# Attention woven into a gated MLP on one core: rounded parts ahead of the gate's functions, exponents gathered

## The chip, the cores and the metric

The kernel runs on one core of a Trainium2 chip. A core has five engines that run their own queues of instructions in order and meet at semaphores: TensorE (PE, matrix products, with its weight loads PEld), VectorE (DVE), ScalarE (ACT, functions read from tables), GpSimd (POOL) and SyncE (SP), which here issues the transfers. The metric is device time in microseconds (us) of one execution; less is better.

## The reference

Sliding-window attention over 8 batches, 8 heads, 576 positions and 64 features, half of the heads dense and half dilated, then a two-layer MLP without bias on the 4608 rows:

```python
scores = scale * np.matmul(q, k.transpose(0, 1, 3, 2))
scores = np.where(masks[None, :, :, :], scores, -1000000000.0)
scores = scores - np.max(scores, axis=-1, keepdims=True)
attn = np.exp(scores)
attn = attn / (np.sum(attn, axis=-1, keepdims=True) + 1e-09)
x = np.matmul(attn, v)          # then (batch, position, head, feature) as 4608 x 512
h = x @ w_in                    # 512 -> 2048
sp = np.maximum(h, 0.0) + np.log1p(np.exp(-np.abs(h)))
g = h * erf(sp)
out = g @ w_out                 # 2048 -> 512
```

## The kernel before

**Attention** is cut into 72 units of four blocks of 64 queries, for two heads at once. A unit passes through: `scores` (PE, 16 small products), `mask_max` (DVE, four, each with a row maximum `nmax`), `exponents` (ACT, four Exp with row sums `ssum`, and one small add on POOL), `normalize` (a reciprocal on DVE, a product on POOL), `transposes` (PE, four) and `turned` (their copy to `pT`), `values` (PE, 16 small products), and then x's two parts: `rows_hi` (ACT: the values rounded to the short matmul format) and `rows_lo` (DVE: the rest). From `scores` of unit n to `values` of unit n are three visits (`LAG = 3`): a visit scores unit n and attends unit n-3.

**The MLP** runs over nine chunks of 512 rows, each in steps of two tiles of 128 hidden features; 72 steps in all, called t. A step is done in two half steps, x = 2t + j. In half step x, PE runs `mm1` (12 products into the one bank `h`), the transposes of units that are due, `mm2` of the step two earlier (12 products into the four banks `acc`), and then values and scores of the units that are due. DVE copies `h` to `hc` (`take`) in each half step. In an odd half step ACT does Erf of the step before (`table`) and then Sigmoid and Ln of its own step (`argument`); each of Erf, Ln and Exp begins with a load of the function table (Sigmoid uses Erf's). DVE makes from Erf's result the two parts of g (`gate`) that the next two half steps' `mm2` read. Besides, weights in double precision are taken apart into two parts, one tile per half step in the first quarter (`prep_act` on ACT, `prep_dve` on DVE; each takes what the other made a half step before).

**Which half step does what** is a fixed plan, `visits()`: the units 0 to 13 are scored before the first `mm1`; 14 to 20 come one to a half step, x = 0 to 6; 21, 22 and 23 at x = 9, 11 and 14; after that two at a time at x = 18, 23, 28, 31, 34, 38, 41, 45 and so on up to 102. The order of instructions within a half step is the order of the calls in the main loop; each engine keeps it. `todo` holds units that are scored and wait for their exponents, `scaled` those that wait for `normalize`. In x = 0 to 3 there is no `mm2` yet, and the transposes come ahead of `mm1`. There the banks `acc` still serve attention: unit u has `acc[(u + 1) % 4]`, so unit 14's values (x = 3) stand in `acc[3]`, which the first `mm2` at x = 4 writes over.

In the profiled execution `mm1` of x = 0, 1, 2, 3, 4, 5 begins at 49.67, 54.09, 59.10, 66.99, 71.87 and 80.37 us, that of x = 8, 9 and 10 at 101.42, 106.86 and 113.99, and that of x = 18 at 162.14.

Of the kernel before, what the change touches and what calls it, by code (L numbers as in the profile page):

```python
# [10 lines left out]
F32 = mybir.dt.float32  # L11
# [7 lines left out]
P = 128  # L19
# [15 lines left out]
PER = 4  # L35
# [26 lines left out]
LAG = 3  # L62
# [40 lines left out]
def key_start(u, j):  # L103

    return j * BLK + (WIN if (PER * u) // NBLK != (PER * u + j) // NBLK else 0)
# [7 lines left out]
def attn_moe_kernel(ctx: ExitStack, tc: tile.TileContext, qk, v, masks, eye, w_in, w_out, out):  # L113
# [3 lines left out]
    def pool(name, bufs, space=bass.MemoryType.SB, **kw):  # L117
        return ctx.enter_context(tc.tile_pool(name=name, bufs=bufs, space=space, **kw))
# [7 lines left out]
    io, work, small = pool("io", 2), pool("work", 2), pool("small", 3)  # L126
# [47 lines left out]
    probs, maxes, sums, x_rows = {}, {}, {}, {}  # L174
# [3 lines left out]
    def scores(u):  # L178
        i = u % 2
        for j in range(PER):  # L180
            at, r = QW + key_start(u, j), j % 2 * BLK
            for h in range(2):
                hs = slice(h * D, (h + 1) * D)
                nc.tensor.matmul(sps[h][r:r + BLK, i, j // 2, :], qkz[i][hs, j * BLK:(j + 1) * BLK],  # L184
                                 qkz[i][hs, at:at + KEYS], start=True, stop=True)

    def mask_max(u):
        pr = probs[u] = work.tile([P, PER, KEYS], F32, name="prob", bufs=LAG + 1)
        nmax = maxes[u] = small.tile([P, PER], F32, name="nmax")
        for h in range(2):  # L190
            for p in range(PER // 2):
                n = PER * u + 2 * p
                nc.vector.tensor_tensor_reduce(  # L193
                    out=pr[:, 2 * h + p, :], in0=sps[h][:, u % 2, p, :], in1=mask[PAIRS.index((kind(n), kind(n + 1)))],
                    scale=-SCALE, scalar=BIG,
                    op0=ALU.add, op1=ALU.min, accum_out=nmax[:, 2 * h + p:2 * h + p + 1],
                )

    def exponents(u):
        nmax = maxes.pop(u)  # L200
        sums[u] = small.tile([P, PER], F32, name="ssum")
        for j in range(PER):
            nc.scalar.activation(  # L203
                out=probs[u][:, j, :], in_=probs[u][:, j, :], func=AF.Exp,
                scale=-1.0, bias=nmax[:, j:j + 1], accum_out=sums[u][:, j:j + 1],
            )
        nc.gpsimd.tensor_scalar(sums[u], sums[u], 1.0e-9, None, op0=ALU.add)
# [20 lines left out]
    def values(u):  # L228
        xp, vt, pt = place(u), vz[u % 2], pz[u in second]
        for j in range(PER):  # L230
            r = j % 2 * BLK
            for h in range(2):
                nc.tensor.matmul(xp[h * D:(h + 1) * D, j * BLK:(j + 1) * BLK], vt[:, j, h, :],  # L233
                                 pt[:, 2 * h + j // 2, r:r + BLK], start=True, stop=True)

    def pieces(u):

# [26 lines left out]
    def rows_hi(u):  # L264
        for hi, _, src in rows_of(u):
            nc.scalar.copy(out=hi, in_=src)  # L266

    def rows_lo(u):

        for hi, lo, src in rows_of(u):  # L270
            nc.vector.tensor_tensor(out=lo, in0=src, in1=hi.bitcast(F32), op=ALU.subtract)  # L271
        for it in [i for i in x_rows if PER * (u + 1) >= NBLK * (i + 1)]:
            b, hp = divmod(it, HP)

            at = slice(TOK if it < twice else 0, TOK if twice <= it < HP else S)

            if HP + twice <= it < 2 * HP:
                whole[it] = x_rows[it]
                at = slice(TOK - (S - TOK), S)
            a = b, hp, at, x_rows.pop(it)  # L280
            if it < HP:
                stores.append(a)
            else:
                soon(store_x, *a)
# [92 lines left out]
    def prep_dve(keep=None):  # L377

        if rest and rest[0][0] < calls[0]:
            _, w, hi, lo = rest.popleft()
            nc.vector.tensor_tensor(lo, w, hi.bitcast(F32), op=ALU.subtract)  # L383
        if begun and begun[0][0] < calls[0]:
            _, i, d, hi, lo, w = begun.popleft()
            t = w.bitcast(I32)
            nc.vector.tensor_scalar(t, t, 3, None, op0=ALU.logical_shift_left)
            nc.vector.scalar_tensor_tensor(t, d[:, :, 1], -0x80000000, t, op0=ALU.bitwise_and, op1=ALU.bitwise_or)  # L388
            nc.vector.scalar_tensor_tensor(t, d[:, :, 0], 29, t, op0=ALU.logical_shift_right, op1=ALU.bitwise_or)  # L389
            made.append((w, hi, lo))  # L390
            if i != keep:
                soon(load_w, i)
# [68 lines left out]
    def table(t):  # L461
        nc.scalar.activation(out=ls[t], in_=ls[t], func=AF.Erf, scale=-1.0)  # L462
# [66 lines left out]
    with tc.manual_schedule():  # L529
        load_qk(0)  # L530
        nc.sync.dma_start(out=cst, in_=masks)
        for t in vz:
            nc.gpsimd.memset(t[KEYS:P], 0.0)
        nc.gpsimd.memset(pz[0][KEYS:P], 0.0)
        load_qk(1)
        nc.sync.dma_start(out=ident, in_=eye)
        for n in range(FIRST):
            if n < 3:
                load_w(n)
            first_visit(n)  # L540
            if 1 <= n <= EARLY:
                prep_dve()
        normalize(FIRST - 2)
        rows_lo(FIRST - 1 - LAG)

        plan = visits()

        pause = 2 * (USED[SPC - 1] + 1) - 2

        late = 3  # L550
        todo, scaled = [], [FIRST - 1]
        for x in range(2 * (NT + 2)):
            t, j = divmod(x, 2)
            ns = plan.get(x, [])
            scored, ready = [n for n in ns if has(n)], [n - LAG for n in ns]
            second.update(ready[1:])

            if t < 2:
                turn(ready)
            if t < NT:  # L560
                after = STEPS[t + 1][0] if ends(t) and t + 1 < NT else None
                if x == 2 * HALF - 4:
                    load_x(1, range(twice))
                elif after and after > 1 and j == 0:
                    load_x(after, range(twice))
                if x in (2 * HALF - 2, SAVED):
                    hold(True)
                mm1(t, j)
                if x == 0:
                    for a in stores:  # L570
                        store_x(*a)
                if after is not None and j == PAIR - 1:
                    load_x(after, range(twice, CC))
                    hold(False)
                take(t, j)

            if j == 0 and x or x == 1:
                for u in todo:
                    exponents(u)
                scaled, todo = scaled + todo, []  # L580
            if j == 1 and 1 <= t <= NT:
                table(t - 1)
            if t >= 2:
                turn(ready)
            if j == 1 and 1 <= t <= NT:
                gate(t - 1, 0)
            if j == 0 and 2 <= t:
                gate(t - 2, 1)
            if j == 1 and t < NT:
                argument(t)  # L590
            if x != pause:
                prep_act()
            if x not in (pause, late):
                prep_dve(keep=2 if SAVED - 4 < x <= SAVED else None)
            if t >= 2:
                mm2(t - 2, j)
                if x == SAVED:
                    save()
                    hold(False)
                    load_w(2)  # L600
                elif ends(t - 2):
                    if j == 1:
                        store(STEPS[t - 2][0])
                    elif STEPS[t - 2][2] == 2:
                        fetch()
            for m in ready:
                values(m)
            for n in scored:
                scores(n)
            for n in ns:  # L610
                soon(load_qk, n + 2)
                soon(load_v, n - 1)
            for n in scored:
                mask_max(n)
                todo.append(n)
            if x == late:
                prep_dve()
            while scaled:
                normalize(scaled.pop(0))
            for m in ready:  # L620
                rows_hi(m)
            for m in ready:
                rows_lo(m)
            if x == SAVED + 2:
                nc.gpsimd.memset(pz[1][KEYS:P], 0.0)
        assert not todo and not prep and not staged and not begun and not made and not rest
# [84 lines left out]
```

## Time and profile before

| | |
|---|---|
| median of 3 runs | 943.34 us (941.51 to 943.72) |
| the profiled execution | 942.44 us, of which the span of the profile is 940.7 |
| PE busy | 915.1 us, 97% |
| ACT busy | 642.5 us, 68% |
| DVE busy | 562.2 us, 60% |
| POOL busy | 82.9 us, 9% |
| granted TensorE clock, mean | 0.997 |

PE is the engine that is nearly always busy, so what the others do counts only where PE waits. The 25.6 us in which PE does nothing are nearly all in the first 85 us. A line of the timeline gives start, duration, engine, line of the kernel, what is written and read, and in brackets how long the engine had been idle and what it waited for.

### The profile page before, as it was taken

How to read it: one execution, taken by the hardware profiler on the slowest of the kernel's cores; microseconds unless marked ns; L12 is line 12 of the kernel's file. 1: busy time of each engine (PE TensorE's matmuls, PEld its weight loads, DVE VectorE, ACT ScalarE, POOL GpSimd, SP SyncE). 2: the span in 40 equal slices, each digit the busy share in tenths (PEclk: the TensorE clock that was granted, in tenths of full speed). 3: DMA queues.
4: the chain of work that ended last, by engine and by line, in shares of the span. 5: the costliest groups of instructions: out<-in, count | busy, mean ns of one | idle time of the engine just before them, and what ended most of it. 6: DMA issues, size and time to landing. Idle time of an engine off the chain costs nothing.

```text
span 940.7 us, 15969 instructions
## 1 busy us (share of the span) xinstructions
PE 915.1 (97%) x6048; PEld 747.8 (80%) x6048; DVE 562.2 (60%) x1511; ACT 642.5 (68%) x1202; POOL 82.9 (9%) x154
## 2 busy tenths in 40 slices
PE   5789999999999999999999999999999999999998
PEld 4567887888888878888888878888888888888886
DVE  6879889886565545555665555555555444335434
ACT  7879888785866866667578657866566555445553
POOL 2321110110100100000000000100000000000000
PEclk9999999999999999999999999999999999999999
DMA  8766444432631242313232152314220302011001
GB/s 277 254 219 222 155 155 136 156 112 94 194 111 67 67 157 67 111 68 116 83 111 73 62 186 103 112 60 132 84 78 34 114 12 79 1 45 45 0 1 45
DMA packets 51500, 98.73 MB, mean 105 GB/s; under 512 B 7136, under 2 KB 20192, under 8 KB 51424
## 3 DMA queue, kind: packets, MB, share of 16 engines
q1 hardware_dynamic: 51136, 97.19, 30.9%
q8 instruction: 48, 0.79, 0.3%
q10 hardware_dynamic: 288, 0.52, 0.1%
q14 instruction: 28, 0.23, 0.1%
HBM read 69.52 MB, written 27.26 MB: 103 GB/s over the span
## 4 chain that ended last, share of the span: by engine, by line
PE 88%; DVE 6%; DMA 3%; ACT 2%; issue 1%; POOL 0%; SPq 0%; POOLq 0%; ACTq 0%; DVEq 0%
PE h L446 40%; PE acc L487 39%; PE tx L233 3%; PE sp L184 3%; PE sp L217 3%; DMA x<-xT 1%; DVE w L388 1%; DVE w L389 1%; DMA qk<-in_qk_dram 1%; DVE prob L193 1%; DVE win_lo L383 1%; PE acc L217 1%; DVE s L469 1%; DMA dbl<-in_w_in_dram 0%; DVE pT L220 0%
## 5 line engine op out<-in xcount | busy, mean ns | idle before, releaser
L454 DVE COPY hc<-h 128x512 f32<-128x512 f32 x144 | 99.5, 691 | 273.5 <-PE h L446 273.1
L446 PE MATMUL h<-x,win_hi 128*128 128x512 f32 x832 | 259.3, 393 | 0.9 <-DMA x<-xT 0.9
L487 PE MATMUL acc<-wout_hi,ghi 128*128 128x512 f32 x576 | 227.5, 395 | 1.2 <-DVE rows L271 1.0
L487 PE MATMUL acc<-wout_lo,ghi 128*128 128x512 f32 x576 | 224.4, 390 | 0.0
L458 ACT ACTIVATE s<-hc 128x1024 f32<-128x1024 f32 x72 | 76.4, 1062 | 184.4 <-DVE hc L454 184.3
L446 PEld LDWEIGHTS h<-x,win_hi 128*128 128x128 f32 x832 | 155.0, 188 | 35.2 <-issue 1.4
L446 PE MATMUL h<-x,win_lo 128*128 128x512 f32 x416 | 162.3, 390 | 0.0
L487 PE MATMUL acc<-wout_hi,glo 128*128 128x512 f32 x576 | 158.8, 389 | 0.0
L487 PEld LDWEIGHTS acc<-wout_hi,ghi 128*128 128x128 f32 x576 | 108.2, 188 | 23.6 <-DVE rows L271 1.4
L487 PEld LDWEIGHTS acc<-wout_hi,glo 128*128 128x128 f32 x576 | 108.1, 188 | 22.6
L487 PEld LDWEIGHTS acc<-wout_lo,ghi 128*128 128x128 f32 x576 | 108.3, 188 | 21.4
L203 ACT ACTIVATE prob<-prob,nmax 128x96 f32<-128x96 f32 x288 | 104.0, 364 | 5.4 <-DVE nmax L193 5.1
L473 DVE TENSOR_TENSOR glo<-s,ghi 128x512 fp32r<-128x512 f32 x144 | 99.7, 693 | 5.1
L459 ACT ACT_TABLE_LOAD x72 | 92.4, 1283 | 1.3
L462 ACT ACT_TABLE_LOAD x72 | 92.4, 1283 | 1.3
L469 DVE TENSOR_TENSOR s<-hc,s 128x1024 f32<-128x1024 f32 x72 | 88.1, 1224 | 7.1 <-ACT s L462 7.1
L446 PEld LDWEIGHTS h<-x,win_lo 128*128 128x128 f32 x416 | 78.3, 188 | 16.7
L193 DVE CUSTOM_DVE_ANT_0 prob<-sp,cst 128x96 f32<-128x96 f32 x288 | 54.8, 253 | 51.8 <-PE sp L184 51.7
L446 PE MATMUL h<-dbl,win_hi 128*128 128x512 f32 x256 | 80.7, 396 | 0.0
L266 ACT CAST rows<-tx 128x64 fp32r<-128x64 f32 (+5 forms) x116 | 26.2, 356 | 75.2 <-PE tx L233 75.2
L462 ACT ACTIVATE s<-s 128x1024 f32<-128x1024 f32 x72 | 76.5, 1062 | 0.8
L459 ACT ACTIVATE s<-s 128x1024 f32<-128x1024 f32 x72 | 76.4, 1061 | 0.8
(59 smaller groups left out, 929.2 us busy)
## 6 DMA issues: line engine op xcount, KB each, us to landing
xT<-rows SPq DMA_DIRECT2D x26, 576.0 KB, 4.7
v<-in_v_dram SPq DMA_DIRECT2D x72, 192.0 KB, 3.8
qk<-in_qk_dram SPq DMA_DIRECT2D x48, 272.0 KB, 3.9
dbl<-in_w_in_dram SPq DMA_DIRECT2D x16, 512.0 KB, 4.2
dbl<-in_w_out_dram SPq DMA_DIRECT2D x16, 512.0 KB, 3.4
qk<-in_qk_dram SPq DMA_DIRECT2D x24, 288.0 KB, 3.9
out_dram<-w SPq DMA_DIRECT2D x26, 256.0 KB, 2.3
x<-xT SPq DMA_DIRECT2D x8, 320.0 KB, 5.2
```

The source lines that it names most:

```text
L184: nc.tensor.matmul(sps[h][r:r + BLK, i, j // 2, :], qkz[i][hs, j * BLK:(j + 1) * BLK], qkz[i][hs, at:at + KEYS], start=True, stop=True)
L193: nc.vector.tensor_tensor_reduce(out=pr[:, 2 * h + p, :], in0=sps[h][:, u % 2, p, :], in1=mask[PAIRS.index((kind(n), kind(n + 1)))], scale ...
L203: nc.scalar.activation(out=probs[u][:, j, :], in_=probs[u][:, j, :], func=AF.Exp, scale=-1.0, bias=nmax[:, j:j + 1], accum_out=sums[u][:, ...
L217: nc.tensor.transpose(out=turn_place(u)[0:KEYS, j * P:(j + 1) * P], in_=pr[:, j, :], identity=ident)
L446: nc.tensor.matmul(h, w[:, cc, ft * P:(ft + 1) * P], x[cc], start=(k == 0 and i == 0), stop=(k == CC - 1 and i == 2))
L454: nc.vector.tensor_copy(out=hs[t][:, j], in_=h)
L458: nc.scalar.activation(out=ls[t], in_=hs[t], func=AF.Sigmoid, scale=-1.0)
L459: nc.scalar.activation(out=ls[t], in_=ls[t], func=AF.Ln, bias=TINY)
L462: nc.scalar.activation(out=ls[t], in_=ls[t], func=AF.Erf, scale=-1.0)
L469: nc.vector.tensor_tensor(out=e, in0=hc, in1=e, op=ALU.mult)
L473: nc.vector.tensor_tensor(out=glo, in0=e[:, j], in1=ghi.bitcast(F32), op=ALU.subtract)
L487: nc.tensor.matmul(acc[tt], g[:, tt * P:(tt + 1) * P], w[:, ft, :], start=(first and w is wout_hi and g is ghi), stop=(last and g is glo))
```

## The change

Four edits. First, a new function `attend` holds values, scores and `rows_hi`, in this order. In x = 0 to 3 it is called right behind `exponents` and `table`, ahead of `gate`, `argument` and `prep_act`; from x = 4 on it stands where values and scores stood. Second, `exponents` run only at an even x at which some waiting unit's transposes are due at x + 2 or earlier (and at x = 1), for all waiting units at once. Third, `prep_dve` of x = 3 goes behind `rows_lo`. Fourth, `nmax` and `ssum` have four buffers and not three.

```diff
-        nmax = maxes[u] = small.tile([P, PER], F32, name="nmax")
+        nmax = maxes[u] = small.tile([P, PER], F32, name="nmax", bufs=LAG + 1)
...
-        sums[u] = small.tile([P, PER], F32, name="ssum")
+        sums[u] = small.tile([P, PER], F32, name="ssum", bufs=LAG + 1)
...
+    def attend(ready, scored):
+        for u in ready:
+            values(u)
+        for u in scored:
+            scores(u)
+        for u in ready:
+            rows_hi(u)
...
+        due = {n - LAG: x for x, ns in plan.items() for n in ns}
...
-            if j == 0 and x or x == 1:
+            if x == 1 or j == 0 and any(due[u] < x + 3 for u in todo):
                 for u in todo:
                     exponents(u)
...
+            if t < 2:
+                attend(ready, scored)
             if t >= 2:
                 turn(ready)
...
-            for m in ready:
-                values(m)
-            for n in scored:
-                scores(n)
+            if t >= 2:
+                attend(ready, scored)
...
-            if x == late:
-                prep_dve()
             while scaled:
                 normalize(scaled.pop(0))
             for m in ready:
-                rows_hi(m)
-            for m in ready:
                 rows_lo(m)
+            if x == late:
+                prep_dve()
```

By the plan the exponents of units 18 and 19 move from x = 6 to x = 8, beside 20; those of 21 and 22 from x = 10 and 12 to x = 16, beside 23. Eight later pairs move by one even half step, from x = 20, 24, 42, 56, 60, 74, 88 and 92 to x + 2. The groups of exponents go from 32 to 29.

On ACT in x = 1 and 2 of before, from the exponents of unit 14 to those of unit 15 (the first line is unit 14's, `rows<-acc_94` is `rows_hi` of unit 12):

```order
L203 ACTIVATE prob,ssum<-prob,nmax 128x96 x4
L458 ACT_TABLE_LOAD
L458 ACTIVATE s<-hc 128x1024
L459 ACT_TABLE_LOAD
L459 ACTIVATE s<-s 128x1024
L369 CAST wout_hi<-w 128x512
L374 ACTIVATE w<-dbl_552 128x512
L266 CAST rows<-acc_94 128x256
L203 ACT_TABLE_LOAD
```

The same place now:

```order
L203 ACTIVATE prob,ssum<-prob,nmax 128x96 x4
L274 CAST rows<-acc_94 128x256
L466 ACT_TABLE_LOAD
L466 ACTIVATE s<-hc 128x1024
L467 ACT_TABLE_LOAD
L467 ACTIVATE s<-s 128x1024
L377 CAST wout_hi<-w 128x512
L382 ACTIVATE w<-dbl_552 128x512
L203 ACT_TABLE_LOAD
```

`rows_hi` of unit 12 has gone from behind Sigmoid, Ln and `prep_act` to the front of them.

On POOL from x = 6 to x = 16 of before (`ssum` is the add of one unit, `prob<-prob,rinv` the product of one unit; the first two rows are units 18 and 19, the four at the end 20 and 21):

```order
L207 TENSOR_SCALAR ssum<-ssum 128x4 x2
L212 TENSOR_TENSOR prob<-prob,rinv 128x384 x2
L425 CAST x_99<-x_99 128x2x64
L425 CAST x_100<-x_100 128x2x64
L207 TENSOR_SCALAR ssum<-ssum 128x4
L212 TENSOR_TENSOR prob<-prob,rinv 128x384
L207 TENSOR_SCALAR ssum<-ssum 128x4
L212 TENSOR_TENSOR prob<-prob,rinv 128x384
```

The same stretch now, with units 18 to 20 and then 21 to 23:

```order
L433 CAST x_99<-x_99 128x2x64
L433 CAST x_100<-x_100 128x2x64
L207 TENSOR_SCALAR ssum<-ssum 128x4 x3
L212 TENSOR_TENSOR prob<-prob,rinv 128x384 x3
L632 MEMSET pT_89 32x512
L207 TENSOR_SCALAR ssum<-ssum 128x4 x3
L212 TENSOR_TENSOR prob<-prob,rinv 128x384 x3
```

Three adds now stand ahead of the first of three products.

## Rows read from the trace of the kernel before

**Rows 1.** The page, busy time, share and instructions of each engine.

```profile
PE 915.1 (97%) x6048; PEld 747.8 (80%) x6048; DVE 562.2 (60%) x1511; ACT 642.5 (68%) x1202; POOL 82.9 (9%) x154
```

**Rows 2.** Busy time by stretches: PE, PEld, DVE, ACT, POOL; PEclk, DMA, GB/s.

```profile
62.00:64.80 2.80, 0.09 (x3) 0.01 (x2) 1.08 (x3) 2.78 (x5) 0.31 (x1) 1.00 0.92 327
64.80:69.00 4.20, 4.20 (x41) 3.52 (x42) 4.13 (x17) 4.17 (x14) 1.09 (x2) 0.59 0.13 39
66.00:67.00 1.00, 1.00 (x14) 0.74 (x9) 0.96 (x2) 1.00 (x6) 0.00 (x0) 0.50 0.00 0
77.00:78.00 1.00, 0.32 (x1) 0.30 (x2) 1.00 (x4) 0.99 (x2) 0.00 (x0) 1.00 0.09 12
100.00:120.00 20.00, 20.00 (x117) 16.26 (x117) 18.07 (x39) 19.04 (x36) 2.27 (x3) 1.00 0.42 143
```

**Rows 3.** PE's timeline: start, duration, line, tiles, idle before and its releaser.

```profile
57.60 0.69 PE L233 MATMUL acc<-pT,v 128*64 128x64 f32 x16 [0.51 <-DVE pT L220]
...
64.79 0.69 PE L233 MATMUL acc<-pT,v 128*64 128x64 f32 x16 [2.71 <-DVE pT L220]
...
77.68 0.50 PE L487 MATMUL acc<-wout_hi,ghi 128*128 128x512 f32 x1 [0.96 <-DVE rows L271]
...
84.09 0.64 PE L217 MATMUL sp<-ident,prob 128*96 128x128 f32 x4 [0.69 <-POOL prob L212]
```

**Rows 4.** ACT's timeline, half steps 1 to 3.

```profile
57.63 1.28 ACT L458 ACT_TABLE_LOAD   x1
...
63.33 0.36 ACT L266 CAST rows<-acc 128x256 fp32r<-128x256 f32 x1
...
69.38 1.06 ACT L462 ACTIVATE s<-s 128x1024 f32<-128x1024 f32 x1
```

**Rows 5.** DVE's timeline, half steps 1 to 4.

```profile
63.72 0.42 DVE L271 TENSOR_TENSOR rows<-acc,rows 128x256 fp32r<-128x256 f32 x1 [2.39 <-ACT rows L266]
...
71.48 1.22 DVE L469 TENSOR_TENSOR s<-hc,s 128x1024 f32<-128x1024 f32 x1
...
82.89 0.24 DVE L211 RECIPROCAL rinv<-ssum 128x4 f32<-128x4 f32 x2
```

**Rows 6.** ACT, POOL and PE around half steps 7 to 9.

```profile
99.62 1.06 ACT L458 ACTIVATE s<-hc 128x1024 f32<-128x1024 f32 x1 [1.16 <-DVE hc L454]
...
106.18 0.36 ACT L203 ACTIVATE prob<-prob,nmax 128x96 f32<-128x96 f32 x1
...
106.54 0.36 ACT L203 ACTIVATE prob<-prob,nmax 128x96 f32<-128x96 f32 x1
106.80 0.19 ACT L203 ACTIVATION_READ_ACCUMULATOR prob<-prob,nmax 128x1 f32 x1
...
107.15 0.68 POOL L207 TENSOR_SCALAR ssum<-ssum 128x4 f32<-128x4 f32 x1 [7.77 <-ACT prob L203]
...
109.58 0.60 PE L217 MATMUL sp<-ident,prob 128*96 128x128 f32 x4
```

**Rows 7.** ACT, DVE and PE in half steps 17 and 18.

```profile
159.33 1.06 ACT L462 ACTIVATE s<-s 128x1024 f32<-128x1024 f32 x1
...
160.42 1.23 DVE L469 TENSOR_TENSOR s<-hc,s 128x1024 f32<-128x1024 f32 x1 [0.27 <-ACT s L462]
...
165.75 1.27 DVE L220 COPY pT<-sp 96x512 f32<-96x512 f32 x2
...
168.40 1.15 PE L233 MATMUL tx<-pT,v 128*64 128x64 f32 x32
```

**Rows 8.** POOL and PE in half steps 30 and 31.

```profile
242.44 0.22 POOL L207 TENSOR_SCALAR ssum<-ssum 128x4 f32<-128x4 f32 x1 [1.20 <-ACT prob L203]
242.74 1.61 POOL L212 TENSOR_TENSOR prob<-prob,rinv 128x384 f32<-128x384 f32 x2
...
244.51 1.03 PE L217 MATMUL sp<-ident,prob 128*96 128x128 f32 x8
```

**Rows 9.** Line by line: the table loads ahead of Exp.

```profile
L203 ACT ACT_TABLE_LOAD x32: 1283/1283/1283, 0.7 to 705.9; - x32
```

## The prediction

> **What bounds the kernel now.** The page comes first: PE works 915.1 of 940.7 us [rows 1], so at most 25.6 us are to be had from PE's waits, and only there. Then busy time by stretches: from 100 us on PE is busy 20.00 of 20 us although ACT is at 19.04 [rows 2], so an ACT instruction saved there brings nothing by itself; it can only cost, where a result comes too late. Third, PE's timeline from the first `mm1` to x = 5: four waits, 0.51, 2.71, 0.96 and 0.69 us [rows 3]. The longest belongs to `values` of unit 13 at x = 2. It waits for `turned` on DVE, which stands behind `rows_lo` of unit 12; that waited 2.39 us for `rows_hi` [rows 5], and `rows_hi` ran at 63.33, because Sigmoid, Ln and `prep_act` had begun at 57.63 ahead of it [rows 4], although the values it reads were done at 57.60 + 0.69 = 58.29 [rows 3]. After this wait the granted clock is 0.50, the 1.2 GHz level, and over 64.8 to 69.0 it is 0.59 on the mean [rows 2]: 4.2 x (1 - 0.59) = 1.7 us lost beside the 2.7 us. The third wait, 0.96 us, is the first `mm2`, whose bank `acc[3]` `rows_lo` of unit 14 still read; the clock stays at 1.00 there [rows 2]. Behind 84.09 PE has hardly a wait; 100 to 120 us shows none [rows 2].
>
> **Edit one, x's parts first (x = 0 to 3).** The 2.71 us wait itself goes: `rows_hi` of unit 12 can start at 58.33 and `rows_lo` right behind the reciprocal, some 2.4 us earlier [rows 5]. But what is late next is ACT. Between 57.63 and the end of Erf of step 0 at 69.38 + 1.06 = 70.44 ACT is busy all the time (2.78 of 2.80 us, 4.17 of 4.20 us) [rows 2, 4]. Now this row of work begins with an instruction that must wait for `values` until 58.33, with Sigmoid, two table loads, Ln, `prep_act` and the exponents of unit 15 queued behind it. The work is the same, it starts 58.33 - 57.63 = 0.70 us later, so Erf ends at 71.14. DVE's product for `gate` of step 0 began at 71.48, held by the copy of `h`, since PE was late [rows 5]; now the copy is early and Erf is what it waits for: 71.18, a gain of 0.3 us. From there to the reciprocals at 82.89 DVE works without a pause on the same instructions in another order (edit three only moves `prep_dve`, 2.4 us, behind `rows_lo`: the 0.96 us wait of `mm2` goes, but the copy of `h` of x = 4 still comes behind both). The reciprocals release POOL's product, and this releases the transposes at 84.09, PE's last wait in this stretch [rows 3]. So they come at 83.79.
>
> PE thus loses the 2.71 and 0.96 us, and waits elsewhere: `prep_dve` of x = 2 needs what `prep_act` of x = 1 makes, now 1.07 us later (0.70, and the 0.36 of `rows_hi` that went ahead), the reciprocal of unit 15 needs exponents that end 0.7 us later, and `turned` of unit 14 is behind both. So I expect new waits for `turned`, of about 2 us each, ahead of `values` of unit 14 and, as DVE gains only 0.3 us, of unit 15. Bounds of edits one and three together: a gain of 6.1 us if all goes (2.71 + 0.96 + 0.69 + 1.7); a loss of 0.7 if the clock falls after the last of these waits: PE's work up to its wait at 84.09 ended at 84.09 - 0.69 = 83.40 [rows 3], now 0.3 earlier and 1.7 longer, 84.8. Without that PE has time until 83.79. I take the chain: **-0.3 us**.
>
> **Edit two, exponents late and together.** Three table loads of 1.283 us go [rows 9], all on ACT, at x = 6, 10 and 12. PE is without a wait there, so I count 0. What it costs, by place:
>
> x = 8, units 18, 19, 20; unit 18's transposes are due at x = 9. Sigmoid of step 3 still starts behind the copy of `h` at 99.62 [rows 6], so the exponents of x = 8 start when they did. One activation takes 0.36 us, start to start; unit 20's four ended at 106.80 + 0.19 = 106.99 [rows 6]. Eight more: 109.87. POOL begins the add 0.16 us later (107.15 behind 106.99): 110.03. The add takes 0.22 us [rows 8] to 0.68 [rows 6]; DVE is idle then, waiting for this very add, so I take 0.22. In POOL's queue the three adds stand before the three products, so unit 18's product has to wait for unit 20's add: 110.03 + 0.30 = 110.33 (from 242.44 to 242.74), and 1.61 / 2 = 0.8 us for one product [rows 8]: 111.15. The transposes stood at 109.58, without a wait [rows 6]; now 111.2: **+1.6 us**, 2.1 with the slower add. Nothing gives it back, since PE is the bound behind it.
>
> x = 16, units 21, 22, 23, due at x = 18. There is time for the transposes, but ACT is 8 x 0.36 = 2.9 us longer and Erf of step 7 stands behind: its end goes from 160.39 to 163.3. DVE's `gate` product waited for it already (0.27 us) [rows 7], and from its start at 160.42 DVE has `gate`, `prep_dve`, the copy of `h` and the two copies `turned` in one row without a pause, the latter at 165.75, two in 1.27 us. All this moves by 2.9: the copies end at 169.3 and 169.95. `values` of the two units ran at 168.40 for 1.15 us; the second half, which began near 168.97, must wait until 170.0: **+1.0 us**.
>
> The eight pairs: seven become due at the next half step. That is what before does in other places: at x = 30 and 31 the second product ends at 244.35 and the transposes start at 244.51 with no wait [rows 8], and the next even x is freed of just this load. 0 each; at x = 22, where `prep_act` still runs, up to 0.2.
>
> **Edit four**, one more buffer of 16 bytes a row for `nmax` and `ssum`: units now wait four deep, no instruction is added. 0.
>
> **Sum:** -0.3 + 1.6 + 1.0 = +2.3 us. On the profiled execution's 942.44 this is 944.7; the median of the runs is 0.9 above it, so **945.6 us**. A change below 0.3%, 2.8 us, can't be told from none here; 2.3 us is just below.
>
> **Rivals.**
>
> *The clock falls at x = 9.* The same two stalls, but PE's pause there, from about 109.7 to 111.2, halves the clock as the 2.71 us at x = 2 did: 1.7 us more, 947.3 us, slower. For it: rows 2 show the fall, and that PE pays it when it is the bound. Against: 0.96 us did not do it, and 1.5 is nearer to that. It decides somewhere between 0.96 and 2.71 us. The Trainium skill (TensorE: Matmul & The Clock Gate, section HAM oscillation — how this bites in real kernels) says that waits between bursts of matmuls drop the array to the low clock and that this is paid anew each time; by that rule every new wait is a risk, and the trace agrees for the one of 2.71 us.
>
> *The stalls are covered.* If ACT, with nothing to do at x = 6, gets ahead after all, or DVE has more slack at x = 18 than I see, only the 0.3 us stay: 943.0 us. For it: with the pairs the plan does the same without a wait [rows 8]. Against: Sigmoid at 99.62 waited 1.16 us for PE [rows 6], so time saved on ACT before it is lost.
>
> *All early waits go.* The gain is 2.71 + 0.96 + 0.69 + 1.7 = 6.1 us, less the stalls' 2.6: 939.8 us, faster. For it: PE waits there for ACT's results, and ACT is what the change relieves. Against: ACT has no gap in 62 to 69 us [rows 2], and no work is taken from it before x = 6. A page of the Trainium skill (ScalarE: Activation LUTs, sections Table sets: the hidden batching unit and What ACT_TABLE_LOAD costs) advises to gather activations by table set and prices a switch at about 2.66 us with the drain; the trace shows 1.283 us [rows 9]. By the page three switches fewer would be 8.0 us on ACT, by the rows 3.85; both would have to reach PE's path, which the stretch from 100 us on speaks against.
>
> **How the numbers follow.** Forecast 0.50, clock 0.16, covered 0.24, all gone 0.10. The forecast's own range is 944.4 to 946.6 (add slower, x = 22; or half a stall less). I take 942.3 to 947.9: above, the clock with the slower add; below, the covered case with the runs' scatter; 939.8 is left out. Faster by over 0.3% (below 940.5) is the last rival: 0.09. Slower by over 0.3% (above 946.2): the clock rival and a third of the forecast, 0.34. The rest, 0.57, is within.
>
> **What would show it.** Right: Erf of step 0 later, not earlier; `values` of unit 13 without a long wait and new waits for `values` of 14 and 15; the transposes of unit 18 waiting some 1.6 us for POOL; `values` at x = 18 waiting 1 us for `turned`; 29 loads ahead of Exp. Wrong: no wait at x = 9 or 18, a clock below 1.00 behind x = 9, or transposes of unit 16 more than 1 us before 84.

## The result, and the profile after

The median of 20 runs is 944.64 us after (942.62 to 946.65) and 942.23 us before (939.95 to 943.72) on the same chip: a ratio of 1.0026, interval 1.0019 to 1.0034. That is 2.4 us more: slower by the interval, and under the 0.3% that the prediction counts as a change, though the interval reaches a little beyond that. The profiled execution has a span of 943.8 us, 3.1 above that of before.

Of the timelines below, only the rows that the text speaks of are shown.

The page after, busy time of each engine; it answers [rows 1].

```profile
PE 915.5 (97%) x6048; PEld 747.7 (79%) x6048; DVE 562.8 (60%) x1511; ACT 638.3 (68%) x1199; POOL 79.0 (8%) x154
```

ACT does what was meant: three instructions and 4.2 us less. PE's work is the same, so the time went into PE's waits. Where, stretch by stretch (columns as in [rows 2]):

```profile
62.00:64.80 2.80, 2.63 (x41) 2.16 (x41) 1.66 (x4) 2.77 (x5) 0.31 (x1) 1.00 0.93 346
64.80:69.00 4.20, 1.98 (x9) 1.31 (x7) 3.59 (x16) 4.17 (x14) 1.05 (x2) 1.00 0.36 129
100.00:120.00 20.00, 18.53 (x110) 14.79 (x110) 16.41 (x38) 19.67 (x43) 3.52 (x6) 1.00 0.40 139
```

PE now works through 62 to 64.8 us, where it stood still, but pauses in 64.8 to 69 us; there the clock stays at 1.00. In 100 to 120 us, where PE had no gap, it now lacks 1.47 us. ACT is busy 98 to 99% in all three.

PE's timeline, its waits from half step 1 to 18, and later transposes as milestones; it answers [rows 3], and PE's rows in [rows 6 to 8].

```profile
57.60 0.69 PE L233 MATMUL acc<-pT,v 128*64 128x64 f32 x16 [0.51 <-DVE pT L220]
...
69.08 0.69 PE L233 MATMUL acc<-pT,v 128*64 128x64 f32 x16 [2.30 <-DVE pT L220]
74.11 0.61 PE L217 MATMUL sp<-ident,prob 128*96 128x128 f32 x4 [0.92 <-DVE nmax L193]
78.62 0.69 PE L233 MATMUL tx<-pT,v 128*64 128x64 f32 x16 [1.12 <-DVE pT L220]
83.84 0.64 PE L217 MATMUL sp<-ident,prob 128*96 128x128 f32 x4 [1.09 <-POOL prob L212]
110.96 0.64 PE L217 MATMUL sp<-ident,prob 128*96 128x128 f32 x4 [1.47 <-POOL prob L212]
...
170.81 1.28 PE L233 MATMUL tx<-pT,v 128*64 128x64 f32 x32 [0.87 <-DVE pT L220]
197.46 1.03 PE L217 MATMUL sp<-ident,prob 128*96 128x128 f32 x8
...
715.51 1.03 PE L217 MATMUL sp<-ident,prob 128*96 128x128 f32 x8
```

The last two, at x = 23 and at the end of the attention, in PE's timeline of before:

```profile
194.92 1.04 PE L217 MATMUL sp<-ident,prob 128*96 128x128 f32 x8
...
712.38 1.03 PE L217 MATMUL sp<-ident,prob 128*96 128x128 f32 x8
```

Both programs have `values` of unit 12 at 57.60, so starts can be subtracted. Transposes of unit 16 (x = 5): 83.84 - 84.09 = -0.25. Of unit 18 (x = 9): 110.96 - 109.58 = +1.38, so 1.63 are lost there. `values` at x = 18 end at 172.09 against 168.40 + 1.15 = 169.55: +2.54, that is the 1.38, another 0.08 at x = 14, at a wait that before has too, and 1.08 that are new at x = 18. x = 23: +2.54. x = 28: 227.70 - 225.15 = +2.55. The last: +3.13. The last 0.58 arises in one place, at a change of tokens (where the MLP goes on to its next 512 rows), where `mm1` waits for x's own transfers, once in before (0.43 us) and twice in after (0.39 us at 354.14, 0.42 at 355.49); the transposes right behind stand at 356.26 against 353.14, +3.12. In the profiles of the experiments that follow, the waits at one such change come to between none and 0.8 us, whatever the edit. I count them as scatter of the transfers.

ACT after; it answers [rows 4], ACT in [rows 6] (Sigmoid of step 3) and [rows 7] (Erf of step 7), with an idle row at x = 6.

```profile
58.34 0.37 ACT L274 CAST rows<-acc 128x256 fp32r<-128x256 f32 x1 [0.72 <-PE acc L233]
...
70.11 1.06 ACT L470 ACTIVATE s<-s 128x1024 f32<-128x1024 f32 x1
...
95.21 0.63 ACT L274 CAST rows<-tx 128x112 fp32r<-128x112 f32 x2 [4.06 <-PE tx L233]
...
99.38 1.06 ACT L466 ACTIVATE s<-hc 128x1024 f32<-128x1024 f32 x1 [1.16 <-DVE hc L462]
...
163.66 1.06 ACT L470 ACTIVATE s<-s 128x1024 f32<-128x1024 f32 x1
```

`rows_hi` of unit 12 runs at 58.34 instead of 63.33, and Erf of step 0 ends 0.73 later, at 71.17. At x = 6, where the first load and exponents went, ACT stands idle for 4.06 us until PE has done `values`; before it waited 0.24 us there.

DVE after, half steps 1 to 5; it answers [rows 5], and the last two rows those of [rows 7].

```profile
71.20 1.23 DVE L477 TENSOR_TENSOR s<-hc,s 128x1024 f32<-128x1024 f32 x1 [1.58 <-ACT s L470]
...
164.76 1.23 DVE L477 TENSOR_TENSOR s<-hc,s 128x1024 f32<-128x1024 f32 x1 [2.39 <-ACT s L470]
...
170.08 1.27 DVE L220 COPY pT<-sp 96x512 f32<-96x512 f32 x2
```

POOL after, at x = 8; it answers POOL in [rows 6, 8]. And the line by line view of [rows 9].

```profile
106.91 0.68 POOL L207 TENSOR_SCALAR ssum<-ssum 128x4 f32<-128x4 f32 x1 [9.32 <-ACT prob L203]
...
109.77 0.22 POOL L207 TENSOR_SCALAR ssum<-ssum 128x4 f32<-128x4 f32 x1 [1.21 <-ACT prob L203]
110.08 2.40 POOL L212 TENSOR_TENSOR prob<-prob,rinv 128x384 f32<-128x384 f32 x3
```

```profile
L203 ACT ACT_TABLE_LOAD  x29: 1283/1283/1283, 0.7 to 709.0; - x29
```

The sums of unit 18 are ready after the first add, at 106.91 + 0.68 = 107.59, and DVE's reciprocal of them is done at 108.32. But POOL takes its instructions in order: the two other adds come ahead of the product, each waiting for four more exponents.

### The profile page after: what moved, and what is told of

It reads as the page before. It is cut to its first block, busy times and chain, and to the rows that moved or that the text cites. A ratio compares the mean times of both kernels' runs of the same rounds, so it can differ in the third digit from the quotient of the medians.

```text
span 943.8 us, 15944 instructions
## 1 busy us (share of the span) xinstructions
PE 915.5 (97%) x6048; PEld 747.7 (79%) x6048; DVE 562.8 (60%) x1511; ACT 638.3 (68%) x1199; POOL 79.0 (8%) x154
## 4 chain that ended last, share of the span: by engine, by line
PE 84%; DVE 6%; ACT 5%; DMA 2%; issue 1%; POOL 1%; SPq 0%; POOLq 0%; DVEq 0%
PE h L454 38%; PE acc L495 37%; PE tx L233 3%; PE sp L184 3%; PE sp L217 2%; ACT prob L203 1%; DMA x<-xT 1%; DVE w L396 1%; DVE win_lo L391 1%; DVE prob L193 1%; DVE w L397 1%; DMA qk<-in_qk_dram 1%; DVE s L477 1%; DVE hc L462 0%; DVE w L395 0%
```

## The experiments

The theory is the prediction's: two stalls, one at x = 9 in POOL's queue, one at x = 18 behind Erf, make the loss, and the early edits return next to nothing. The rival is that the 2.4 us lie elsewhere: in the early stretch, in a fallen clock, or in the pairs of units that now come due at the next half step. Each median has 9 to 11 runs. E1 to E4 ran beside before with 942.58 us, E5 to E7 with 942.51.

**E1, x's parts alone.** Edits one and three stay; the exponents run at every even x again.

```diff
-        due = {n - LAG: x for x, ns in plan.items() for n in ns}
...
-            if x == 1 or j == 0 and any(due[u] < x + 3 for u in todo):
+            if j == 0 and x or x == 1:
```

> The first and third edit alone (x's parts first in x = 0 to 3, prep_dve of x = 3 behind rows_lo); exponents at every even half step as before. Theory (two late-exponent stalls of 1.6 and 1.0 us, early edits worth 0.3 us): ratio to before 0.9997, transposes of unit 16 at 83.8 us, the four early waits of PE in their new places (about 2.3, 0.9, 1.1, 1.1 us), no wait at x = 9 and at x = 18. Rival (the new early waits, 5.4 us in sum against 4.9, are what costs): ratio 1.002 or more, and the transposes of unit 16 later than 84.1.

942.03 us, ratio 1.0003 (0.9992 to 1.0015): nothing that can be told from before, and under the 1.002 of the rival. PE's timeline:

```profile
58.04 0.69 PE L233 MATMUL acc<-pT,v 128*64 128x64 f32 x16 [0.50 <-DVE pT L220]
69.52 1.12 PE L233 MATMUL acc<-pT,v 128*64 128x64 f32 x16 [2.30 <-DVE pT L220]
84.29 0.64 PE L217 MATMUL sp<-ident,prob 128*96 128x128 f32 x4 [1.10 <-POOL prob L212]
...
194.60 1.03 PE L217 MATMUL sp<-ident,prob 128*96 128x128 f32 x8
```

The early stretch is that of after, with its 2.30 us wait; at x = 9 there is no wait. The first row stands 0.44 later than in before, so the transposes of unit 16 come 84.29 - 0.44 - 84.09 = 0.24 earlier, as in after. Here the clock did fall behind the 2.30 us: the same 16 matmuls take 1.12 us instead of 0.69. It moved nothing at unit 16.

**E2, the exponents alone.** Edits two and four stay; `values`, `scores` and x's parts go back to where they were.

```diff
-    def attend(ready, scored):
...
-            if t < 2:
-                attend(ready, scored)
...
-            if t >= 2:
-                attend(ready, scored)
+            for m in ready:
+                values(m)
+            for n in scored:
+                scores(n)
...
+            if x == late:
+                prep_dve()
             while scaled:
                 normalize(scaled.pop(0))
             for m in ready:
+                rows_hi(m)
+            for m in ready:
                 rows_lo(m)
-            if x == late:
-                prep_dve()
```

> The second edit alone (exponents as late as the plan allows, together), with the buffers it needs; x's parts where they were before. Theory: +2.6 us, ratio 1.0028; transposes of unit 16 at 84.1 as before, unit 18's wait 1.5 us for POOL's product, values at x = 18 wait 0.9 us for the copies. Rival (early waits cost): ratio 1.0005 or less, no such waits of over 0.5 us.

944.22 us, ratio 1.0023 (1.0011 to 1.0035): the whole loss. PE's timeline:

```profile
58.36 0.69 PE L233 MATMUL acc<-pT,v 128*64 128x64 f32 x16 [0.51 <-DVE pT L220]
65.54 1.13 PE L233 MATMUL acc<-pT,v 128*64 128x64 f32 x16 [2.68 <-DVE pT L220]
84.68 0.64 PE L217 MATMUL sp<-ident,prob 128*96 128x128 f32 x4 [0.70 <-POOL prob L212]
111.78 0.64 PE L217 MATMUL sp<-ident,prob 128*96 128x128 f32 x4 [1.47 <-POOL prob L212]
171.65 1.28 PE L233 MATMUL tx<-pT,v 128*64 128x64 f32 x32 [0.86 <-DVE pT L220]
```

Both stalls are there, 1.47 and 0.86 us, behind an early stretch like that of before. So the loss belongs to the exponents, and the order of x's parts neither makes nor softens it. The row at 84.68 also shows how far one profile differs from another: with the first half steps of before, unit 16's transposes come (84.09 - 57.60) - (84.68 - 58.36) = 0.17 earlier than in before's profile.

**E3, POOL's adds between its products.** As after, but for units 18 to 23 the add stands ahead of its own product. ACT's work is the same.

```diff
-        nc.gpsimd.tensor_scalar(sums[u], sums[u], 1.0e-9, None, op0=ALU.add)
+        if not 18 <= u < 24:
+            nc.gpsimd.tensor_scalar(sums[u], sums[u], 1.0e-9, None, op0=ALU.add)

     def normalize(u):
+        if 18 <= u < 24:
+            nc.gpsimd.tensor_scalar(sums[u], sums[u], 1.0e-9, None, op0=ALU.add)
```

> The changed kernel, with POOL's adds of units 18 to 23 issued between the products (add 18, product 18, add 19, ...) and not all in front. ACT's order is unchanged. Theory (unit 18's product waits for unit 20's add only through POOL's order): the transposes at x = 9 start right behind mm1, no wait over 0.2 us, so 1.5 us less than the changed kernel, ratio 1.0010; the 0.9 us at x = 18 stay. Rival (the longer ACT row itself holds PE at x = 9, by Erf or the reciprocals on DVE): the wait moves to mm2 or values and the ratio stays at 1.0026.

944.23 us, ratio 1.0017 (1.0008 to 1.0027), between the 1.0010 of the theory and the 1.0026 of the rival; the runs alone don't tell it from after. POOL's and DVE's timelines, then PE's:

```profile
108.72 0.83 POOL L215 TENSOR_TENSOR prob<-prob,rinv 128x384 f32<-128x384 f32 x1 [0.82 <-DVE rinv L214]
...
119.16 0.68 DVE L465 COPY hc<-h 128x512 f32<-128x512 f32 x1
```

```profile
57.93 0.69 PE L236 MATMUL acc<-pT,v 128*64 128x64 f32 x16 [0.51 <-DVE pT L223]
109.64 0.60 PE L220 MATMUL sp<-ident,prob 128*96 128x128 f32 x4
119.90 0.50 PE L457 MATMUL h<-wout_hi,win_hi 128*128 128x512 f32 x1
145.37 0.69 PE L236 MATMUL tx<-pT,v 128*64 128x64 f32 x16 [1.03 <-DVE pT L223]
...
196.96 1.03 PE L220 MATMUL sp<-ident,prob 128*96 128x128 f32 x8
```

Counted from the first row, unit 18's product starts (110.08 - 57.60) - (108.72 - 57.93) = 1.69 us earlier, and the stall at x = 9 is gone, with the same exponents: the queue's order made it. But only half comes through. In the same count this kernel is 1.65 us ahead of after at x = 9, (110.96 - 57.60) - (109.64 - 57.93), and 0.83 at x = 23. PE, now earlier, meets what the stall had hidden. The eight exponents that moved to x = 8 also stand ahead of Erf of step 3, so DVE's product for `gate` waits for it until 113.39, and DVE works in one row from there to the copy of `h` of x = 10. That copy ends at 119.84, and `mm1` of x = 11, which writes the same bank `h`, begins at 119.90; in before the copy ended at 117.75 and `mm1` began at 119.58 without a wait. Up to the transposes of x = 11 this costs 0.4 us. The other 0.4 come at x = 14, where the wait is 1.03 instead of 0.61 us: half of it because the transfer of weights behind that wait is issued 0.24 later, with DVE still late, half because it takes 0.20 longer (last section), which I count as scatter. So the rival of this experiment is true in part: the longer row of ACT does hold PE, but at x = 11 and not at x = 9.

**E4, unit 23's exponents apart.** As after, but units 21 and 22 at x = 12 and unit 23 alone at x = 16.

```diff
-            if x == 1 or j == 0 and any(due[u] < x + 3 for u in todo):
+            if x in (1, 12, 16) or j == 0 and any(due[u] < x + 3 for u in todo):
```

> The changed kernel, with the exponents of units 21 and 22 at x = 12 and unit 23 alone at x = 16 (one table load more). Theory (8 exponents more ahead of Erf of step 7 make gate, prep_dve and the copies at x = 18 2.9 us late): the wait of values at x = 18 goes, 1.0 us less than the changed kernel, ratio 1.0015 to 1.0017; the 1.5 us at x = 9 stay. Rival (the wait at x = 18 is carried over from the delay at x = 9): it stays, ratio 1.0026.

944.31 us, ratio 1.0015 (1.0003 to 1.0026), as foreseen, though the runs alone don't tell it from after. PE's timeline:

```profile
111.57 0.64 PE L217 MATMUL sp<-ident,prob 128*96 128x128 f32 x4 [1.47 <-POOL prob L212]
166.84 1.04 PE L217 MATMUL sp<-ident,prob 128*96 128x128 f32 x8
197.06 1.03 PE L217 MATMUL sp<-ident,prob 128*96 128x128 f32 x8
```

The stall at x = 9 stays, that at x = 18 is gone: from the transposes of units 21 and 22 to the next, PE takes 30.22 us as in before (164.70 to 194.92); after takes 31.30 (166.16 to 197.46). That is the 1.08.

**E5, E3 and E4 together.** What is left of edit two is the eight pairs, and two of its three saved loads.

> The changed kernel with both remedies at once: POOL's adds of units 18 to 23 between the products, and units 21 and 22 at x = 12, 23 at x = 16; the units 18 to 20 together at x = 8 and all later pairs stay as late as in the changed kernel. Theory (two stalls are the whole loss, and the pairs cost nothing): no wait at x = 9 and x = 18, only 0.4 to 1.0 us at x = 14, where the run with the adds between gave 0.4 back; ratio 1.0000 to 1.0004. Rival (the late pairs or the fewer loads have a price of their own): 1.0010 or more, with waits behind x = 20.

943.40 us, ratio 1.0011 (0.9999 to 1.0024). PE's timeline:

```profile
58.18 0.69 PE L236 MATMUL acc<-pT,v 128*64 128x64 f32 x16 [0.51 <-DVE pT L223]
109.88 0.60 PE L220 MATMUL sp<-ident,prob 128*96 128x128 f32 x4
...
195.90 1.04 PE L220 MATMUL sp<-ident,prob 128*96 128x128 f32 x8
```

By the trace, against before and from the first row: -0.28 at x = 9, +0.40 at x = 14 (where PE waits 0.85 us), +0.40 at x = 23 and at x = 28. So the late pairs cost nothing up to there, and 0.4 us of the loss remain by x = 14. They come as in E3: the copy of `h` of x = 10 ends at 120.08, `mm1` of x = 11 begins at 120.13, and the transposes of x = 11 stand at +0.10. So the batch at x = 8 costs PE's path some 0.6 us, from -0.28 to +0.40 less 0.08 for a transfer, even without the stall in POOL's queue. The median is 0.9 us above before's, nearer to the rival's 1.0010 than to the theory's 1.0004; the interval holds both, so the runs agree with the trace's 0.4, but don't show it.

**E6, x's parts between Sigmoid and Ln.** E1, with `rows_hi` at x = 1 a place later, so that ACT doesn't start on an instruction that waits.

```diff
-    def attend(ready, scored):
+    def attend(ready, scored, parts=True):
...
-        for u in ready:
+        for u in ready if parts else ():
             rows_hi(u)
...
         nc.scalar.activation(out=ls[t], in_=hs[t], func=AF.Sigmoid, scale=-1.0)
+        for u in between:
+            rows_hi(u)
         nc.scalar.activation(out=ls[t], in_=ls[t], func=AF.Ln, bias=TINY)
...
-                attend(ready, scored)
+                attend(ready, scored, x != 1)
...
-                argument(t)
+                argument(t, ready if x == 1 else ())
```

> First and third edit, exponents as in the kernel before, but in x = 1 rows_hi of unit 12 stands between Sigmoid and Ln and not ahead of Sigmoid's table load. Theory (the early edits gained only 0.25 us because ACT's row of work starts 0.7 us later, at the end of the values): Erf of step 0 ends at 70.4 and not at 71.1, the transposes of unit 16 come at 83.1 to 83.2 and not at 83.8, 0.7 us less than x's parts first alone; ratio 0.9990 to 0.9996. Rival (DVE alone holds this stretch): Erf is earlier, the transposes of unit 16 stay at 83.8.

942.22 us, ratio 0.9994 (0.9985 to 1.0003). Erf of step 0 in ACT's timeline, then PE's:

```profile
69.46 1.06 ACT L472 ACTIVATE s<-s 128x1024 f32<-128x1024 f32 x1
```

```profile
57.77 0.69 PE L233 MATMUL acc<-pT,v 128*64 128x64 f32 x16 [0.51 <-DVE pT L220]
68.43 0.69 PE L233 MATMUL acc<-pT,v 128*64 128x64 f32 x16 [1.47 <-DVE pT L220]
83.20 0.64 PE L217 MATMUL sp<-ident,prob 128*96 128x128 f32 x4 [1.10 <-POOL prob L212]
```

Taking out ACT's 0.72 us of waiting moves Erf's end to 70.52 and the 2.30 us wait to 1.47. Unit 16's transposes come 84.09 - (83.20 - 0.17) = 1.06 earlier. That the row of ACT's work, not the place of x's parts on PE, set the early stretch is shown by the trace; the runs only lean to faster.

**E7, no weights prepared at x = 3.** E6, and of `prep_act` and `prep_dve` the pause moves from x = 22 to x = 3.

```diff
-            if x != pause:
+            if x != late:
                 prep_act()
-            if x not in (pause, late):
+            if x != late:
                 prep_dve(keep=2 if SAVED - 4 < x <= SAVED else None)
...
-            if x == late:
-                prep_dve()
```

> The same, and the half step x = 3 takes no weights apart (neither on ACT nor on DVE); the half step x = 22, which left them out, does it instead, so the same tiles are made. Theory (from Erf of step 0 on, DVE works without a pause to the transposes of unit 16, and 2.4 us of that are prep_dve of x = 3): the transposes of unit 16 come at 80 to 81, PE's waits in x = 4 and 5 nearly go; 3 us less than the kernel before, ratio 0.996 to 0.998 (worse if tiles that come half a step later make PE wait elsewhere). Rival (ACT or the transfers hold this stretch): the transposes stay near 83, ratio 0.999 or more.

939.95 us, ratio 0.9973 (0.9962 to 0.9985): faster than before by 2.6 us, and by the two ratios 0.5% faster than after. PE's timeline:

```profile
59.12 0.69 PE L233 MATMUL acc<-pT,v 128*64 128x64 f32 x16 [0.51 <-DVE pT L220]
69.78 0.69 PE L233 MATMUL acc<-pT,v 128*64 128x64 f32 x16 [1.47 <-DVE pT L220]
82.16 0.64 PE L217 MATMUL sp<-ident,prob 128*96 128x128 f32 x4
142.91 0.69 PE L233 MATMUL tx<-pT,v 128*64 128x64 f32 x16 [1.03 <-DVE pT L220]
```

POOL's product is no longer late at x = 5: the transposes of unit 16 come without a wait, 84.09 - (82.16 - 1.52) = 3.45 earlier. A longer wait at x = 14, 1.03 us instead of 0.57, takes 0.46 back; the transfer behind it took 0.50 longer here (last section).

**All of them beside the trace.** The time from the start of `values` of unit 12 to that of the transposes at x = 23 in each profile, against before's 194.92 - 57.60 = 137.32. What comes ahead of x = 1 is left out of this count; its first row stands between 57.60 and 59.12 in the nine profiles.

| kernel | in the trace, us | the runs, ratio |
|---|---|---|
| after | +2.54 | 1.0026 (1.0019 to 1.0034) |
| E1 parts alone | -0.76 | 1.0003 (0.9992 to 1.0015) |
| E2 exponents alone | +2.66 | 1.0023 (1.0011 to 1.0035) |
| E3 adds between | +1.71 | 1.0017 (1.0008 to 1.0027) |
| E4 split at 16 | +1.54 | 1.0015 (1.0003 to 1.0026) |
| E5 both | +0.40 | 1.0011 (0.9999 to 1.0024) |
| E6 behind Sigmoid | -0.94 | 0.9994 (0.9985 to 1.0003) |
| E7 no weights at 3 | -3.00 | 0.9973 (0.9962 to 0.9985) |

Divided by 942.5 each trace falls into its interval (E1, 0.9992, on its edge). The order of the kernels is nearly that of the trace, so the loss lies between x = 1 and x = 23. E1's -0.76 holds 0.49 that x = 14 spared it by a quicker transfer (last section), which says nothing of the edit.

## Why the prediction was right

**x's parts first, -0.3 us forecast, -0.25 measured.** The size says little, as E2 has 0.17 of it without the edit; the five profiles with the edit in this form have -0.23 to -0.25. The chain is what bears the step out, and it held at each link: Erf ended at 71.17 (71.14 foreseen), DVE's product began at 71.20 (71.18), the transposes at 83.84 (83.79). That the 2.71 and 0.96 us waits go and return elsewhere held too, but not in the sizes: 2.30 us ahead of unit 14's `values`, then 1.12 instead of 2 ahead of unit 15's, and between them 0.92 us that I had not seen, the transposes of unit 15 waiting for `mask_max` of unit 17. It made no difference, since POOL's product at x = 5 ended later than either. E6 shows the 0.70 us on ACT that the step rests on: with them taken out, the transposes come 0.81 earlier than in after. As to the room for such steps: of the 25.6 us in which PE does nothing in before, 20.2 lie in the first 85 us and 3.9 in the last 10.7.

**The stall at x = 9, +1.6 forecast, +1.63 measured.** The last add ran at 109.77 and the products began at 110.08, 0.25 earlier than foreseen, because Sigmoid came 0.24 earlier with the early gain; the rest is as worked out. E3 shows that POOL's order is the cause of this stall. What the step didn't ask is what else the eight exponents hold up: Erf of step 3, and by it DVE, which the stall hid in after (DVE's product waited 0.77 us for Erf there). So a repair of POOL's order is worth half in E3, and some 0.6 us of the batch's price remain in E5.

**The stall at x = 18, +1.0 forecast, +1.08 measured.** On after's clock, 1.46 us late by then, Erf ended at 164.72 - 1.46 = 163.26 (163.3 foreseen). The shape was a little off: 0.87 of it is a wait ahead of the first matmul, not in the middle. E4 shows its cause. The prediction has all three units of this batch due at x = 18; unit 23 is due at x = 23 only, and was in it because it waited too, which changes nothing in the sum.

**Three loads for nothing.** 29 loads, 4.2 us less ACT, and none of it reached PE: ACT's idle time at x = 6 grew from 0.24 to 4.06 us. The pairs cost 0: the offset is +2.54 at x = 18 and x = 23, +2.55 from x = 28 to the change of tokens and +3.12 to +3.14 behind it.

**The sum** was +2.3 us, and the trace has 2.54 by x = 28. The medians differ by 2.41. That the two agree to 0.1 us is luck: 0.2 us early and up to 0.8 us at a change of tokens come and go between profiles. The forecast of 945.6 is 1.0 above the median of the 20 runs, since it stood on three runs of before with a median 1.1 us higher.

**The rivals.** The clock did not fall at x = 9: behind the 1.47 us wait it reads 1.00 throughout 100 to 120 us. The Trainium skill (TensorE: Matmul & The Clock Gate, section HAM oscillation — how this bites in real kernels) has long waits between bursts of matmuls drop the clock, and each time anew; these runs agree for the 2.71 and 2.68 us waits and, in one profile of five with a wait of 2.28 or 2.30 us, for that one; behind the five waits of 1.47 us it stayed. The covered case fell with the two stalls. "All early waits go" fell for the reason given, that ACT has no gap there; E7 shows what it takes: work taken from x = 3 itself, for 3.45 us at x = 5. The prediction let the length of the wait decide, somewhere between 0.96 and 2.71 us; at 2.28 to 2.30 us it went either way. One bound was too dark: I priced a fallen clock in the early stretch at 0.7 us, and in E1 it fell and cost nothing at unit 16, since the slack ahead of the waits for `turned` of unit 15 and POOL's product, 1.12 and 1.09 us in after, was larger than I had counted.

The Trainium skill (ScalarE: Activation LUTs, section Table sets: the hidden batching unit) advises to gather activations by table set. ACT did gain the loads' time, 3 x 1.283 = 3.85 of its 4.2 us; PE's path lost 2.7 by the batches of three, and the runs decide for the path.

## What to carry to other kernels

Before gathering work to save switches on an engine that is not the bound, ask for each batch when its first member is needed: the first result of a batch leaves no earlier than the order of the queue behind it allows, and here two batches of three units cost 2.7 us that three saved switches could not pay. In an engine's in-order queue, put each unit's small step next to the large step that it feeds, and ask what else stands behind the batch: with POOL's order mended, Erf was still late, and half of the gain was gone. And where an early row of waits ends in one late engine, moving the waits brings nothing; moving work out of that half step does.

## What the runs showed of the hardware

The clock does not answer to the length of a wait alone. The wait of 2.28 to 2.30 us at x = 3 stands in the profiles of after, E1, E3, E4 and E5; the stretch of 69.5 to 75 us behind it has these rows in E1 and in E4:

```profile
69.50:75.00 5.50, 5.48 (x45) 4.39 (x46) 3.84 (x14) 5.46 (x8) 0.00 (x0) 0.69 0.83 291
```

```profile
69.50:75.00 5.50, 4.42 (x47) 3.41 (x48) 3.85 (x15) 5.46 (x8) 0.00 (x0) 1.00 0.82 294
```

The clocks in these rows, 0.69 and 1.00, are borne out by the matmuls: `values` of unit 14, 16 of them, took 1.12 us in E1 and 0.69 us in E4.

In the first 45 us that column can't be read so. In 20 to 40 us of before it says 1.00:

```profile
20.00:40.00 20.00, 16.19 (x200) 11.98 (x196) 19.66 (x88) 17.39 (x67) 5.87 (x12) 1.00 0.78 264
```

E1 has 0.59 in the same stretch. Yet 16 matmuls of `values` take 1.12 us at 20.55 in before as they do at 20.35 in E1, the time that they take with the clock fallen behind the 2.30 us in E1, and 0.69 us only from 45.28 on in before. So these matmuls ran at the low level, 1.2 GHz, there in both; the difference in the column is none in the matmuls, and a mean of 0.997 for the whole of before can't hold this stretch. Where a clock matters, compare the duration of the same matmuls as well.

The wait at x = 14, 0.57 to 1.03 us in most profiles and none in E1, hangs on the transfer of weights issued behind the saved result at x = 11. From its issue to ACT's `prep_act` it took 4.28 us in before, 4.34 in after, 4.54 in E3, 4.78 in E7 and 3.82 in E1. From the transposes to `values` at x = 14, PE took 3.95 us in before, 4.41 in E7 and 3.46 in E1, so each moved with the transfer. Some 0.5 us of difference to before, either way, can be that alone.
